# Rows loaded first, reciprocal roots on GpSimd, and the shift table built during the statistics, in a gated long-convolution and token-MLP kernel

## The chip, the cores and the metric

The kernel runs on one core of a Trainium2 chip. The metric is the device time of one execution in microseconds (us). "Span" is the time between the first and the last instruction in a profile; it is about 1.8 us shorter than the device time. The engines are TensorE (PE in the profile, with PEld for its weight loads), VectorE (DVE), ScalarE (ACT), GpSimd (POOL) and the DMA queues.

## The reference, cut to what matters

```python
# S = 2048 positions, D = 640 channels, F = 1536 hidden units, bf16
g = sigmoid((q * gate_w).sum(-1, keepdims=True))

# A: four shift taps, a product, a convolution over all S positions, a product
kv = shift4(k, shift_k) * v            # shift_k is (640, 4)
y  = irfft(rfft(pad(kv)) * rfft(pad(ssm_k)))[:S] + kv * ssm_D
a  = q * y

# B: layer norm over channels, then an MLP over positions
h = (q - mean(q)) / sqrt(var(q) + 1e-5)
u = gelu(einsum("bsd,sf->bdf", h, w1) + b1)
b = (einsum("bdf,fs->bds", u, w2) + b2).transpose(0, 2, 1)

out = g * a + (1 - g) * b
```

## The kernel before

The Fourier transforms are matrix products with a cosine and sine table `FTB`, which ScalarE makes at the start. The order of the work on TensorE: first come 40 transposes of the convolution filter (`transp`, first half of the positions), then 64 matmuls that transform it ("filter transforms", `fwd`, name W). The same follows for the second half. Then 80 matmuls apply the shift taps to `k`, and 128 transform the result ("convolution transforms", name A). Then come the rest of the MLP and the inverse transforms. Whenever nothing of this is ready, the matmuls of the first MLP layer (`m1`, priority 10^6, 384 of 128x320 in groups of 8) serve as filler. They need normalised rows `X`.

Instructions are ordered when the kernel is built, by a list scheduler that models the engines. A smaller `prio` goes first. PSUM is cut into four slots; the transforms may hold three, the MLP two. Each group of four transform matmuls ends in an eviction of 128x640 from PSUM by ScalarE, and only then is its slot free again.

```python
x_load(0)                                   # rows of q
for hk in range(2):
    ssm_load(hk)                            # filter rows
small(Drow...); small(rows... shift_k); small(rows... b2); small(rows... b1)
x_load(1); w1_load(0, 0); ssm_load(2); ssm_load(3); x_load(2); w1_load(0, 1); x_load(3)
# ...
SC.add("POOL", 1.3, lambda s: T.op("POOL", lambda e: e.tensor_copy(ro, ri), ...), name="taps")
# ... one PSUM tile takes b2, b1 and the turned taps (name "cst"), ScalarE takes them out (cc, cw)

def transp(h, p, kt):                       # 5 transposes, then one eviction
    # ...
    mms(vt, items, name="wtr")
    act(wT[:, hk, p, :], full, ACT.Copy, vt=vt, name="wT")

def fwd(src, h, p, dst, slot, scale, name, ...):
    for k2 in range(2):
        for c in range(2):
            # ... 4 matmuls of 128x320, then one eviction
            mms(vt, items, name=name)
            act(o, two, ACT.Copy, vt=vt, name=name + "e", **kw)

def ln_scale(a, b):                         # 1/sqrt by an integer guess and three Newton steps
    def emit(s):
        op(... ALU.add 1e-5); op(... logical_shift_right); op(... ALU.mult, ALU.add)
        for _ in range(3):
            op(scalar_tensor_tensor); op(tensor_tensor); op(scalar_tensor_tensor)
        op(... ALU.mult)
    return SC.add("DVE", 1.5, emit, ..., prio=0, name="rstd")

for h in range(2):
    for p in PORD:
        for kt in range(2):
            transp(h, p, kt)
    for p in PORD:
        fwd(srcW(h), h, p, C[h], p, 1.0 / 1024.0, "W", ...)
    if h == 0:
        for a, b in ((0, 8), (8, 16)):      # two halves of 8 row tiles
            for t in range(a, b):
                ln_tile(t // 4, t % 4)      # statistics: bn_stats twice, bn_aggr once
            ln_scale(a, b)                  # root
            ln_apply(a, b)                  # (x - mean) * rstd
        for g0 in (0, 5, 10, 15):           # the shift table KF, four multiplies
            tt("POOL", KF[...], V(cw, ...), V(m32, ...), ALU.mult)
        # ...
# ...
for ft in range(FT):                        # first MLP layer: the filler
    for hk in range(4):
        mms(vt, items, prio=10 ** 6 + 4 * ft + hk, name="m1")     # 8 matmuls
    g_ = act(GT[:, ft, :]..., two, ACT.Gelu_apprx_tanh, ..., vt=vt, prio=0, name="gelu")
```

## Time and profile before

| | before |
|---|---|
| time, median of 4 runs | 193.47 us (193.34 to 193.65) |
| span of the profiled run | 191.6 us |
| TensorE busy | 177.6 us, 93% |
| VectorE busy | 179.6 us, 94% |
| ScalarE busy | 116.3 us, 61% |

Two lines of the page come first: the busy time of each engine, and the shares of the chain of waits that ended last.

```profile
PE 177.6 (93%) x1403; PEld 130.0 (68%) x1403; DVE 179.6 (94%) x221; ACT 116.3 (61%) x187; POOL 26.8 (14%) x28
...
PE 58%; DVE 29%; ACT 10%; issue 1%; POOL 0%; DVEq 0%; POOLq 0%
```

Both TensorE and VectorE look full. The chain gives VectorE 29% of the span, and the change takes time from VectorE.

The next fence is VectorE's timeline around the first root. Its columns are start, duration, engine, line, operation, output and inputs, shapes and count; what an engine waited for stands in brackets.

```profile
13.90 0.84 DVE L862 BATCH_NORM_STATS2 stats<-X 128x6 f32<-128x320 bf16 x2
...
15.49 2.06 DVE L874 TENSOR_SCALAR sd<-mv 128x8 f32<-128x8 f32 x1
17.58 1.99 DVE L875 TENSOR_SCALAR rstd<-sd 128x8 int32<-128x8 int32 x1
19.61 1.99 DVE L876 TENSOR_SCALAR rstd<-rstd 128x8 int32<-128x8 int32 x1
21.63 0.17 DVE L878 SCALAR_TENSOR_TENSOR gth<-rstd 128x8 f32<-128x8 f32 x1
...
23.52 2.94 DVE L637 TENSOR_SCALAR X<-X,mv,rstd 128x640 bf16<-128x640 bf16 x8
...
41.47 2.94 DVE L637 TENSOR_SCALAR X<-X,mv,rstd 128x640 bf16<-128x640 bf16 x8
```

Three operations on eight numbers per partition take 2 us each, and the fourth takes 0.17 us. GpSimd's timeline shows what ran beside them:

```profile
4.98 3.31 POOL L776 COPY rows<-rows 20x512 bf16<-20x512 bf16 x1 [3.13 <-DMA rows<-in_A_shift_k_dram]
...
13.43 8.14 POOL L622 TENSOR_TENSOR KF<-cw,m 128x1120 bf16<-128x1120 bf16 x4 [5.15 <-ACT cw L666]
```

The four table multiplies take about 2.04 us each, from 13.43 to 21.57, and each of the three slow operations of VectorE ends with one of them. They took 2.0 us beside the multiplies, where the same three operations of the second root, with no multiply beside them, took 0.17 us each (37.56 to 38.14). The statistics keep their 0.42 us beside the first multiply (two in 0.84), as before it (two in 0.83 to 0.84). Why the ones take longer beside a multiply and the others don't, no run here shows.

The last view is a table of stretches. Each row has the stretch, its length, then busy time and count of instructions for PE, PEld, DVE, ACT and POOL, then TensorE's recorded clock, the DMA share and GB/s.

```profile
7.06:14.07 7.01, 5.30 (x49) 4.28 (x49) 7.01 (x24) 6.79 (x14) 1.86 (x2) 1.00 1.08 373
14.07:25.91 11.84, 11.51 (x72) 6.40 (x73) 11.36 (x25) 10.30 (x17) 7.50 (x4) 1.00 1.05 383
25.91:30.58 4.67, 4.06 (x50) 3.12 (x48) 4.67 (x13) 4.44 (x8) 0.00 (x0) 1.00 0.58 121
30.58:40.22 9.64, 9.64 (x65) 4.98 (x65) 9.23 (x32) 9.64 (x17) 0.87 (x1) 1.00 1.03 287
40.22:44.39 4.17, 4.15 (x82) 3.98 (x82) 4.17 (x10) 4.17 (x6) 0.00 (x0) 1.00 1.00 411
44.39:51.54 7.15, 5.87 (x47) 4.02 (x43) 7.15 (x9) 4.36 (x7) 0.00 (x0) 1.00 0.50 121
```

The rows are, in order: first transposes, first filter transforms with 8 filler matmuls, second transposes with 8, second filter transforms, shift taps, and 40 fillers with 2 convolution matmuls. The rest of the convolution transforms begins at 51.54. In a dense stretch of the second MLP product 320 matmuls take 43.63 us, 0.136 us each; a transpose or a shift-tap matmul takes about 0.054 us at full pace (80 shift-tap matmuls in 4.33 us). Call the length of a stretch minus its matmuls at these paces "lost". From 7.06 to 51.54 there are 186 large matmuls and 160 small ones, so 44.48 - 186 x 0.136 - 160 x 0.054 = 10.5 us are lost. This is the amount that the change could work on.

### The profile page before, as it was taken

The page shows a single profiled execution, that of the slowest core. Times are in us where ns is not written, and L with a number is a line of the kernel's source. Part 1 is how long each engine was busy: PE and PEld are TensorE (multiplying, and loading weights), DVE is VectorE, ACT ScalarE, POOL GpSimd, SP SyncE. Part 2 cuts the span into 40 slices and gives each one's busy share as a digit, 9 for nine tenths or more (in the row PEclk, how much of TensorE's full clock was granted, in tenths as well). Part 3 has the DMA queues.
Part 4 walks back from the last instruction along what each step waited for, and adds up shares of the span by engine and source line. Part 5 has one row for each costly group of instructions (what it writes and reads, how often), then busy time and mean ns, then how long its engine had stood idle before and what let it go on. Part 6 is the DMA issues. An engine that isn't in the chain of part 4 may idle for free.

```text
span 191.6 us, 3381 instructions
## 1 busy us (share of the span) xinstructions
PE 177.6 (93%) x1403; PEld 130.0 (68%) x1403; DVE 179.6 (94%) x221; ACT 116.3 (61%) x187; POOL 26.8 (14%) x28
## 2 busy tenths in 40 slices
PE   1469999999799999999999999999999999999993
PEld 0456465577466975777777777888888887777672
DVE  7999999999999999999999999999999996599764
ACT  4899979999399999998211221131313132874662
POOL 2619500100000405000002310405000000000000
PEclk9999999999999999999999999999999999999999
DMA  5999959994799199999929766698998900032233
GB/s 187 358 353 389 396 175 210 288 409 187 146 206 350 31 197 285 240 230 318 178 59 280 142 117 177 198 195 195 231 223 248 362 11 0 3 131 74 74 137 137
DMA packets 37295, 38.93 MB, mean 203 GB/s; under 512 B 15643, under 2 KB 32672, under 8 KB 37280
## 3 DMA queue, kind: packets, MB, share of 16 engines
q1 hardware_dynamic: 34464, 32.15, 54.9%
q0 software_dynamic: 2752, 6.55, 19.0%
q8 instruction: 11, 0.18, 0.3%
q14 instruction: 4, 0.03, 0.0%
q10 hardware_dynamic: 64, 0.01, 0.0%
HBM read 25.87 MB, written 2.62 MB: 149 GB/s over the span
## 4 chain that ended last, share of the span: by engine, by line
PE 58%; DVE 29%; ACT 10%; issue 1%; POOL 0%; DVEq 0%; POOLq 0%
PE pp L293 58%; DVE stats L862 6%; ACT C L666 3%; DVE C L622 3%; DVE SS L622 3%; DVE X L637 3%; ACT ksh L666 2%; ACT gq L666 2%; DVE pint L636 2%; DVE kp L735 2%; DVE vkv L622 1%; DVE pint L622 1%; ACT cgb L666 1%; DVE rstd L875 1%; DVE rstd L876 1%
## 5 line engine op out<-in xcount | busy, mean ns | idle before, releaser
L293 PE MATMUL pp<-X,ring 128*128 128x320 bf16 x384 | 53.8, 299 | 0.3 <-DVE X L637 0.3
L293 PE MATMUL pp<-GT,W 128*128 128x320 bf16 x384 | 53.3, 299 | 0.1
L293 PEld LDWEIGHTS pp<-GT,W 128*128 128x128 bf16 x384 | 43.5, 113 | 9.1 <-ACT cgb L666 0.4
L622 DVE TENSOR_TENSOR C<-C 128x2560 bf16<-128x2560 bf16 (+1 forms) x28 | 49.2, 1774 | 0.1
L293 PEld LDWEIGHTS pp<-X,ring 128*128 128x128 bf16 x384 | 37.1, 98 | 15.3 <-DVE X L637 0.7
L666 ACT ACTIVATE C<-pp 128x640 bf16<-128x640 f32 x64 | 39.3, 770 | 5.0 <-PE pp L293 4.8
L666 ACT ACTIVATE O<-pp,c,omg 128x640 bf16<-128x640 f32 (+1 forms) x17 | 14.5, 852 | 33.2 <-PE pp L293 33.2
L666 ACT ACTIVATE GT<-pp,cc 128x640 bf16<-128x640 f32 x12 | 9.6, 802 | 21.9 <-PE pp L293 21.8
L622 DVE TENSOR_TENSOR tm<-C,C 128x2560 bf16<-128x2560 bf16 (+2 forms) x12 | 20.2, 1709 | 0.5 <-DMA C<-tm 0.4
L293 PE MATMUL pp<-wT,FTB 128*128 128x320 bf16 x128 | 20.1, 311 | 0.6 <-ACT wT L666 0.4
L666 ACT ACTIVATE cgb<-pp,gg 128x640 bf16<-128x640 f32 x16 | 12.7, 792 | 7.7 <-PE pp L293 7.0
L293 PEld LDWEIGHTS pp<-wT,FTB 128*128 128x128 bf16 x128 | 10.8, 101 | 9.4 <-ACT C L666 4.4
L622 DVE TENSOR_TENSOR C<-tm 128x2560 bf16<-128x2560 bf16 (+1 forms) x12 | 14.9, 1265 | 0.1
L293 PE MATMUL pp<-C,GTB 128*128 128x320 bf16 x96 | 14.1, 299 | 0.0
L862 DVE BATCH_NORM_STATS2 stats<-X 128x6 f32<-128x320 bf16 x32 | 13.7, 472 | 0.0
L262 POOL DMA_DIRECT2D C<-C x6 | 7.4, 1390 | 43.5 <-DVE C L622 43.4
L666 ACT ACTIVATE gq<-gq 128x640 bf16<-128x640 bf16 x16 | 12.0, 777 | 0.0
L293 PEld LDWEIGHTS pp<-C,GTB 128*128 128x128 bf16 x96 | 9.0, 98 | 4.2 <-ACT O L666 0.8
L293 PE MATMUL pp<-ident,ssm 128*128 128x128 bf16 x80 | 8.0, 265 | 4.0 <-DMA ssm<-in_A_ssm_k_dram 3.4
L622 DVE TENSOR_TENSOR tm<-C,SS 128x5120 bf16<-128x5120 bf16 x4 | 11.1, 2818 | 0.0
L293 PE MATMUL pp<-vkv,FTB 128*128 128x320 bf16 x64 | 9.5, 300 | 1.3 <-DVE vkv L622 1.3
L293 PEld LDWEIGHTS pp<-ident,ssm 128*128 128x128 bf16 x80 | 6.5, 128 | 5.7 <-DMA ssm<-in_A_ssm_k_dram 4.2
(68 smaller groups left out, 182.8 us busy)
## 6 DMA issues: line engine op xcount, KB each, us to landing
ring<-in_B_w_dram SPq DMA_DIRECT2D x12, 512.0 KB, 9.5
W<-in_B_w_dram SPq DMA_DIRECT2D x8, 768.0 KB, 6.2
C<-C POOLq DMA_DIRECT2D x6, 640.0 KB, 10.0
X<-in_A_q_dram SPq DMA_DIRECT2D x4, 640.0 KB, 9.3
ssm<-in_A_ssm_k_dram SPq DMA_DIRECT2D x4, 640.0 KB, 8.9
kn<-in_A_k_dram SPq DMA_DIRECT2D x4, 640.0 KB, 9.3
out_dram<-O SPq DMA_DIRECT2D x7, 320.0 KB, 2.3
vkv<-in_A_v_dram SPq DMA_DIRECT2D x2, 640.0 KB, 4.6
```

The source lines that it names most:

```text
L262: ins = engobj.dma_start(out_ap, in_ap, accum_op=ALU.add, max_dma_last_dim=2560)
L293: ins = self.nc.tensor.matmul(ps_ap, lhsT=lhsT, rhs=rhs, start=start, stop=stop, skip_group_check=True)
L622: o_ = SC.add(eng, d, lambda s: T.op(eng, lambda e: e.tensor_tensor(o, a, b, op), [a, b], [o]), [a, b], [o], prio=prio, name="tt")
L636: return e.tensor_scalar(o, a, s1, None, op0=op0)
L637: return e.tensor_scalar(o, a, s1, s2, op0=op0, op1=op1)
L666: return T.op("ACT", lambda e: e.activation(o, src, func, **kw), rr + [src], ww)
L735: SC.add("DVE", 0.75, lambda s: T.op("DVE", lambda e: e.tensor_copy(ov, iv), [i[:, :, :]], [o[:, :, :]]), [i[:, :, :]], [o[:, :, :]], prio ...
L862: SC.add("DVE", 0.38, (lambda o, i: lambda s: T.op("DVE", lambda e: e.bn_stats(o, i), [i], [o]))(o, i), [i], [o])
L875: op(lambda e: e.tensor_scalar(yi, vi, 1, None, op0=ALU.logical_shift_right), [vi], yi)
L876: op(lambda e: e.tensor_scalar(yi, yi, -1.0, float(0x5F3759DF), op0=ALU.mult, op1=ALU.add), [yi], yi)
```

## The change

The intent is to give VectorE its 8 us back and to have normalised rows early, so that filler exists sooner. The rows of `q` are loaded before the weights. GpSimd computes the roots with a power operation. Twelve tiles, four of them of the second half, get their statistics before the first apply; the last four follow it, and then comes the second root. VectorE turns the taps. The taps get a PSUM tile of their own with top priority, so the table build on GpSimd runs beside the statistics, which kept their 0.42 us beside a multiply in before.

```diff
-            d = dve_dur(n, mode) + extra if eng == "DVE" else n / 900.0 + 0.3
+            d = dve_dur(n, mode) + extra if eng == "DVE" else n / 900.0 + 0.2
@@ loads
+        small(rows[0:20, 0, 0:128], dr(A_shift_k, ...), 5120, "QA")
+        small(rows[0:4, 1, :], dr(B_b2, ...), 4096, "QA")
+        small(rows[0:12, 2, 0:128], dr(B_b1, ...), 3072, "QA")
+        small(Drow[:, :], dr(A_ssm_D, ...), 1280, "QA")
         x_load(0)
         for hk in range(2):
             ssm_load(hk)
-        small(Drow...); small(rows... shift_k); small(rows... b2); small(rows... b1)
-        x_load(1)
-        w1_load(0, 0)
+        for hk in range(1, 4):
+            x_load(hk)
         ssm_load(2)
         ssm_load(3)
-        x_load(2)
+        w1_load(0, 0)
         w1_load(0, 1)
-        x_load(3)
@@ taps and table
-        SC.add("POOL", 1.3, lambda s: T.op("POOL", lambda e: e.tensor_copy(ro, ri), ...), name="taps")
+        SC.add("DVE", 0.6, lambda s: T.op("DVE", lambda e: e.tensor_copy(ro, ri), ...), prio=0, name="taps")
-        # b2, b1 and the taps in one PSUM tile: mms(vt, items, name="cst")
+        # the taps alone:                      mms(vt, items, prio=0, name="cst")
-            act(V(cw, ...), ..., name="cw")
+            act(V(cw, ...), ..., prio=0, name="cw")
+        def consts():                          # b2 and b1, called after the first transposes
@@ roots
         def ln_scale(a, b):
-            # 13 operations on VectorE (shown above)
+            n = b - a
+            ts("POOL", sd[:, a:b], mv[:, a:b, 1], 1e-5, None, ALU.add, prio=0)
+            tt("POOL", rstd[:, a:b], sd[:, a:b], V(cst, 1, [[0, n]]), ALU.pow, prio=0).dur = 1.05
+            return tt("POOL", sd[:, a:b], sd[:, a:b], rstd[:, a:b], ALU.mult, prio=0)
@@ order
-                for a, b in LNG:
-                    for t in range(a, b):
-                        ln_tile(t // 4, t % 4)
-                    ln_scale(a, b)
-                    ln_apply(a, b)
+                for t in range(12):
+                    ln_tile(t // 4, t % 4)
+                ln_scale(0, 8)
+                ln_apply(0, 8)
+                for t in range(12, 16):
+                    ln_tile(t // 4, t % 4)     # after the first apply
+                ln_scale(8, 16)
+                ln_apply(8, 16)
# cut: the lists that keep this order (lnlast), the same for the mixing products
```

More of the change, by code (lines that the diff above doesn't have):

```diff
@@ L748, in small @@
             dma(o, i, nbytes, stream=stream, **kw)
+        small(rows[0:20, 0, 0:128], dr(A_shift_k, 0, [[128, 20], [1, 128]]), 5120, "QA")
+        small(rows[0:4, 1, :], dr(B_b2, 0, [[512, 4], [1, 512]]), 4096, "QA")
+        small(rows[0:12, 2, 0:128], dr(B_b1, 0, [[128, 12], [1, 128]]), 3072, "QA")
+        small(Drow[:, :], dr(A_ssm_D, 0, [[0, 1], [1, D]]), 1280, "QA")
         x_load(0)
@@ L752, in _build @@
             ssm_load(hk)
-        small(Drow[:, :], dr(A_ssm_D, 0, [[0, 1], [1, D]]), 1280, "QA")
-        small(rows[0:20, 0, 0:128], dr(A_shift_k, 0, [[128, 20], [1, 128]]), 5120, "QA")
-        small(rows[0:4, 1, :], dr(B_b2, 0, [[512, 4], [1, 512]]), 4096, "QA")
-        small(rows[0:12, 2, 0:128], dr(B_b1, 0, [[128, 12], [1, 128]]), 3072, "QA")
-        x_load(1)
-        w1_load(0, 0)
+        for hk in range(1, 4):
+            x_load(hk)
         ssm_load(2)
         ssm_load(3)
-        x_load(2)
+        w1_load(0, 0)
         w1_load(0, 1)
-        x_load(3)
         T_PI = float(np.float32(math.pi * (1.0 - 1e-6)))
@@ L775, in _build @@
         ro, ri = rows[0:20, 3, :].rearrange("g (j q c) -> g j q c", j=4, q=4), V(rows, 0, [[1, 4], [0, 4], [4, 32]], pn=20)
-        SC.add("POOL", 1.3, lambda s: T.op("POOL", lambda e: e.tensor_copy(ro, ri), [ri], [ro]), [ri], [ro], name="taps")
+        SC.add("DVE", 0.6, lambda s: T.op("DVE", lambda e: e.tensor_copy(ro, ri), [ri], [ro]), [ri], [ro], prio=0, name="taps")
         PORD = (0, 2, 1, 3)
@@ L794, in _build @@
         items = []
-        for p in range(4):
-            items.append(((lambda s, p=p: s[:, 4 * p:4 + 4 * p]), V(rows, 512 + p, [[4, 128]], pn=4), ident[0:4, 0:4], True, True))
-        items.append(((lambda s: s[:, 16:28]), rows[0:12, 2, 0:128], ident[0:12, 0:12], True, True))
         for j in range(4):
             items.append(((lambda s, j=j: s[:, 512 + 20 * j:512 + 20 * j + 20]), rows[0:20, 3, 128 * j:128 * j + 128], ident[0:20, 0:20], True, True))
-        mms(vt, items, name="cst")
-        act(cc[:, :], lambda s: s[:, 0:28], ACT.Copy, vt=vt, name="cc")
+        mms(vt, items, prio=0, name="cst")
         for q in range(4):
-            act(V(cw, q, [[7, NG], [1, 4]], p0=32 * q, pn=32), (lambda s, q=q: s[32 * q:32 * q + 32, 512:592].rearrange("p (j g) -> p g j", j=4)), ACT.Copy, vt=vt, name="cw")
+            act(V(cw, q, [[7, NG], [1, 4]], p0=32 * q, pn=32), (lambda s, q=q: s[32 * q:32 * q + 32, 512:592].rearrange("p (j g) -> p g j", j=4)), ACT.Copy, vt=vt, prio=0, name="cw")
         b2f = V(cc, 0, [[1, 4], [4, 4]])
@@ L806, in _build @@
         ts("DVE", m32[:, :], dif2[:, :], 0.0, None, ALU.is_equal, mode=2)
+        def consts():
+            vt = _VT("cv")
+            items = []
+            for p in range(4):
+                items.append(((lambda s, p=p: s[:, 4 * p:4 + 4 * p]), V(rows, 512 + p, [[4, 128]], pn=4), ident[0:4, 0:4], True, True))
+            items.append(((lambda s: s[:, 16:28]), rows[0:12, 2, 0:128], ident[0:12, 0:12], True, True))
+            mms(vt, items, name="cst")
+            act(cc[:, :], lambda s: s[:, 0:28], ACT.Copy, vt=vt, name="cc")
         def transp(h, p, kt):
@@ L837, in tt @@
             def tt(*a):
-                return tt_(*a, prio=prio)
+                o_ = tt_(*a, prio=prio)
+                if prio is not None:
+                    o_.after.update(lnlast[-1:])
+                return o_
             def sl(h, s, n=1):
@@ L859, in ln_tile @@
             xs = X[:, hk, p, :]
+            ops = []
             for ci in range(2):
                 o, i = stats[:, t, 6 * ci:6 * ci + 6], xs[:, 320 * ci:320 * ci + 320]
-                SC.add("DVE", 0.38, (lambda o, i: lambda s: T.op("DVE", lambda e: e.bn_stats(o, i), [i], [o]))(o, i), [i], [o])
+                ops.append(SC.add("DVE", 0.38, (lambda o, i: lambda s: T.op("DVE", lambda e: e.bn_stats(o, i), [i], [o]))(o, i), [i], [o]))
             o, i = mv[:, t, :], stats[:, t, :]
-            SC.add("DVE", 0.12, (lambda o, i: lambda s: T.op("DVE", lambda e: e.bn_aggr(o, i), [i], [o]))(o, i), [i], [o])
+            ops.append(SC.add("DVE", 0.12, (lambda o, i: lambda s: T.op("DVE", lambda e: e.bn_aggr(o, i), [i], [o]))(o, i), [i], [o]))
+            return ops
         def ln_scale(a, b):
-            v, y, z, m_ = sd[:, a:b], rstd[:, a:b], gth[:, a:b], mv[:, a:b, 1]
-            yi = y.bitcast(I32)
-            vi = v.bitcast(I32)
-            def emit(s):
-                def op(fn, rr, w):
-                    T.op("DVE", fn, rr, [w])
-                op(lambda e: e.tensor_scalar(v, m_, 1e-5, None, op0=ALU.add), [m_], v)
-                op(lambda e: e.tensor_scalar(yi, vi, 1, None, op0=ALU.logical_shift_right), [vi], yi)
-                op(lambda e: e.tensor_scalar(yi, yi, -1.0, float(0x5F3759DF), op0=ALU.mult, op1=ALU.add), [yi], yi)
-                for _ in range(3):
-                    op(lambda e: e.scalar_tensor_tensor(out=z, in0=y, scalar=-0.5, in1=y, op0=ALU.mult, op1=ALU.mult), [y], z)
-                    op(lambda e: e.tensor_tensor(z, z, v, ALU.mult), [z, v], z)
-                    op(lambda e: e.scalar_tensor_tensor(out=y, in0=z, scalar=1.5, in1=y, op0=ALU.add, op1=ALU.mult), [z, y], y)
-                op(lambda e: e.tensor_tensor(v, v, y, ALU.mult), [v, y], v)
-            return SC.add("DVE", 1.5, emit, [m_], [v, y, z], prio=0, name="rstd")
+            n = b - a
+            ts("POOL", sd[:, a:b], mv[:, a:b, 1], 1e-5, None, ALU.add, prio=0)
+            tt("POOL", rstd[:, a:b], sd[:, a:b], V(cst, 1, [[0, n]]), ALU.pow, prio=0).dur = 1.05
+            return tt("POOL", sd[:, a:b], sd[:, a:b], rstd[:, a:b], ALU.mult, prio=0)
         def ln_apply(a, b):
@@ L886, in ln_apply @@
                 xs = X[:, t // 4, t % 4, :]
-                ts("DVE", xs, xs, mv[:, t, 0:1], rstd[:, t:t + 1], ALU.subtract, ALU.mult, mode=4, extra=0.16, prio=1)
+                o_ = ts("DVE", xs, xs, mv[:, t, 0:1], rstd[:, t:t + 1], ALU.subtract, ALU.mult, mode=4, extra=0.16, prio=1)
+                o_.after.update(lnlast[-1:])
         MIXP = 330
-        LNG = ((0, 8), (8, 16))
+        LNA = 8
+        lnlast = []
         KFP = (0, 5, 10, 15)
@@ L896, in _build @@
                     transp(h, p, kt)
+            if h == 0:
+                consts()
             for p in PORD:
@@ L899, in _build @@
             if h == 0:
-                for a, b in LNG:
-                    for t in range(a, b):
-                        ln_tile(t // 4, t % 4)
-                    ln_scale(a, b)
-                    ln_apply(a, b)
+                for t in range(8):
+                    ln_tile(t // 4, t % 4)
+                for t in range(8, 12):
+                    ln_tile(t // 4, t % 4)
+                lnlast.append(SC.ops[-1])
+                ln_scale(0, LNA)
+                ln_apply(0, LNA)
+                lnlast.append(SC.ops[-1])
+                for t in range(12, 16):
+                    for o_ in ln_tile(t // 4, t % 4):
+                        o_.after.update(lnlast[-1:])
+                ln_scale(LNA, 16)
+                ln_apply(LNA, 16)
+                lnlast.append(SC.ops[-1])
                 for g0 in KFP:
```

## The prediction

> **What bounds it now.** The timeline shows TensorE without a gap from 51.5 to 188.4 us; by the table of stretches it is busy 136.4 of those 136.9 us, at a granted clock of 1.00. 320 matmuls of the second MLP product take 43.6 us there (0.136 us each), so that stretch is TensorE at its pace. The last 3.2 us are ScalarE, VectorE and the output DMA. What can be won lies before 51.5 us. Matmuls started there: 80 weight transposes (about 0.054 us each), 128 filter transforms, some 58 MLP matmuls, 80 of the shift convolution: about 34 us of work at those paces in the 44.5 us since 7.06 us, when the first filter rows landed. So some 10 us are lost, nearly all because ScalarE evacuates slowly (0.61 us per transform group, 0.63 per transpose group) or because normalised rows, the filler, are not there.
>
> VectorE is busy 94% and never waits from 1 to 112 us. In its timeline the first root (adds, integer steps, three Newton rounds on 128x8) takes 8.0 us, 15.5 to 23.5: three of its 13 operations last 2.0 us each, against 0.17 us in the second root. They end as GpSimd's four shift-table multiplies end (2.06 us each, 13.4 to 21.6). Batch statistics beside the first multiply kept their 0.43 us. [...]
>
> **The change, on VectorE.** Removed: 8.0 us and 2.5 us of roots. Added: the shift-tap turn, estimated 0.6 us from the 0.82 us strided key copies. GpSimd's 3.3 us turn, behind which a small operation lasted 0.67 us, goes. The table build moves to about 8.7 to 17 us, under statistics, and costs nothing. The first half's root is hidden behind four more statistics tiles (0.86 us each); the second's is exposed, I guess 1 to 2 us (no power on GpSimd is in this trace), partly filled by a key turn. First apply: 18.6 instead of 23.5 us; second: 27.5 instead of 41.5. VectorE runs 8 to 9 us ahead.
>
> **On ScalarE.** The four table evictions (1.0 us) move into its idle time near 6.3 us. Its gap at 24.8 to 26.1 and the 3.2 us wait before 52.0 mostly close.
>
> **On the critical path.** The convolution's transforms now start at 51.5, after a VectorE product; ScalarE's own work (about 39.5 us from 7.4) would allow 47 to 48. First-layer matmuls must fill the gaps as well as the 5.4 us they filled at 44.4 to 49.8. They can start near 20 us, when the weights (now later in the queue) land, but until about 28 only 16 exist, so the transposes near 24 to 28 stay half empty. I expect 3 to 5 of the 10 us back. VectorE's 8 to 9 us of lead is mostly not time: TensorE stays the limit, with the same 3 us tail.
>
> **Predicted 189.6 us, 187.4 to 191.8 eight times in ten.** Faster by over 2%: 0.51; within 2%: 0.47; slower: 0.02.
>
> **To check.** Statistics still 0.43 us beside the table build; no 2 us tiny operations; both applies begin near 18.6 and 27.5; convolution transforms begin at 46 to 49; TensorE dense until 183 to 185; tail near 3 us.
>
> **What would make it wrong.** GpSimd's power taking several microseconds, [...]; the fixed instruction order making an engine wait for a DMA that lands later than planned (weights after all rows); TensorE fillers starving ScalarE, so that only 1 us comes back; or VectorE's lead letting the inverse transforms finish early and shorten the tail as well, for a gain above 6 us.

## The result, and the profile after

| | before | after |
|---|---|---|
| time, median of 4 runs | 193.47 us | 191.88 us (191.66 to 192.32) |
| span of the profiled run | 191.6 us | 190.1 us |
| convolution transforms begin in earnest | 51.54 | 52.96 |
| large matmuls done before that | 186 | 200 |
| lost on TensorE from the first transpose to there | 10.5 us | 9.8 us |
| end of TensorE | 188.38 | 187.00 |

The ratio of after to before is 0.992, with a 95% interval of 0.990 to 0.994. A ratio is the mean time of one kernel's runs over that of the other's of the same rounds, so it isn't quite the ratio of the medians quoted here. Executions over 1.5% slower than the fastest of the same kernel are left out of the means. The kernel became 0.8% faster; 2% had been given a chance of one half. All outputs are right. The page of after:

```profile
PE 175.9 (93%) x1403; PEld 131.2 (69%) x1403; DVE 170.3 (90%) x196; ACT 116.8 (61%) x187; POOL 33.5 (18%) x33
...
PE 86%; ACT 9%; DMA 3%; issue 0%; SPq 0%; DVE 0%
```

VectorE lost 9.3 us of busy time, and it left the chain. TensorE's share of the chain rose from 58% to 86%, and yet the span fell by only 1.5 us. VectorE's timeline after:

```profile
13.77 0.82 DVE L870 BATCH_NORM_STATS2 stats<-X 128x6 f32<-128x320 bf16 x2
...
18.99 2.94 DVE L637 TENSOR_SCALAR X<-X,mv,rstd 128x640 bf16<-128x640 bf16 x8 [0.26 <-POOL rstd L622]
...
28.99 2.94 DVE L637 TENSOR_SCALAR X<-X,mv,rstd 128x640 bf16<-128x640 bf16 x8 [2.11 <-POOL rstd L622]
...
45.28 0.23 DVE L636 TENSOR_SCALAR gpre<-mv,gws 128x16 f32<-128x16 f32 x1 [3.41 <-ACT gq L666]
```

The first apply came 4.5 us earlier and the second 12.5 us. Part of the lead turned into waiting: 2.11 us for the second root, and 3.41 us at 45.28 for a ScalarE sum queued behind the first Gelu. GpSimd's timeline after:

```profile
8.83 8.14 POOL L622 TENSOR_TENSOR KF<-cw,m 128x1120 bf16<-128x1120 bf16 x4 [6.97 <-ACT wT L666]
16.95 0.25 POOL L636 TENSOR_SCALAR sd<-mv 128x8 f32<-128x8 f32 x1
17.27 1.68 POOL L622 TENSOR_TENSOR rstd<-sd,cst 128x8 f32<-128x8 f32 x1
...
33.94 6.53 POOL L967 COPY KT<-KT 128x20 bf16<-128x20 bf16 x1 [4.70 <-DMA KT<-kp]
```

The table is built from 8.83 to 16.97, beside statistics that still take 0.41 us each. The power operation took 1.68 us on 128x8. VectorE's part of the change therefore worked as intended. The stretches of after, in the same order as before:

```profile
7.28:14.43 7.15, 4.87 (x47) 3.77 (x48) 7.15 (x25) 6.39 (x10) 5.60 (x3) 0.98 1.04 401
14.43:26.01 11.58, 11.58 (x72) 7.14 (x73) 11.28 (x37) 9.58 (x17) 4.64 (x5) 0.86 1.07 364
26.01:31.00 4.99, 4.30 (x50) 3.22 (x49) 2.88 (x9) 4.75 (x9) 2.11 (x3) 1.00 1.07 183
31.00:44.44 13.44, 12.38 (x88) 8.04 (x89) 10.84 (x10) 12.76 (x21) 6.53 (x1) 1.00 0.98 330
44.44:48.62 4.18, 4.16 (x83) 3.98 (x81) 3.34 (x5) 3.99 (x7) 0.00 (x0) 1.00 0.01 2
48.62:52.96 4.34, 4.34 (x36) 3.12 (x33) 4.34 (x4) 3.77 (x8) 0.00 (x0) 1.00 1.01 139
```

Look at the second filter transforms, the row that starts at 31.00. They now hold 24 fillers (88 matmuls, not 64). That is 3.3 us of work at 0.136 us each, and the row grew from 9.64 to 13.44 us, by 3.8 us. Lost time in this row rose from 0.9 to 1.5 us (13.44 - 88 x 0.136). In the last row the loss went from 1.4 us to nothing. The first three rows hardly moved: 4.85 to 5.0, 2.05 to 1.8, 1.4 to 1.75. From 7.28 to 52.96 there are 200 large and 160 small matmuls, so 45.68 - 27.2 - 8.64 = 9.8 us are lost.

The end of TensorE moved by 1.38 us, and the sum closes. It lost 0.7 us less before the convolution transforms and 0.90 us less after them (136.84 us from 51.54 to 188.38 in before, 134.04 us from 52.96 to 187.00 in after, where 14 large matmuls fewer are left: 136.84 - 134.04 - 14 x 0.136), and it started 0.22 us later. Of the 0.90 us, 0.32 us is one wait for an eviction at 72.90, gone in after; the rest is spread out, and I did not trace it.

The timeline of ScalarE in after shows what the fillers did to it:

```profile
25.12 1.90 ACT L666 ACTIVATE C<-pp 128x640 bf16<-128x640 f32 x3 [0.65 <-PE pp L293]
...
35.17 4.28 ACT L666 ACTIVATE C<-pp 128x640 bf16<-128x640 f32 x7 [0.65 <-PE pp L293]
39.47 1.28 ACT L666 ACT_TABLE_LOAD   x1
40.77 0.79 ACT L666 ACTIVATE GT<-pp,cc 128x640 bf16<-128x640 f32 x1
41.46 3.07 ACT L666 ACTIVATE C<-pp 128x640 bf16<-128x640 f32 x5
```

Each time TensorE runs 8 fillers (1.09 us) in the middle of the transforms, ScalarE runs dry for 0.65 us. A transform group takes TensorE 4 x 0.136 = 0.545 us and ScalarE about 0.605 us, so ScalarE is the slower one, but only by a tenth, and at most three slots lie between them. Also, the four early filler groups complete the first hidden block in the middle of these evictions, so its Gelu now stands there with its table load: 2.07 us from 39.47 to 41.46. TensorE then waits once:

```profile
42.21 1.31 PE L293 MATMUL pp<-wT,FTB 128*128 128x320 bf16 x8 [1.06 <-ACT C L666]
...
52.96 4.01 PE L293 MATMUL pp<-vkv,FTB 128*128 128x320 bf16 x28
```

In before it waited elsewhere:

```profile
51.54 3.75 PE L293 MATMUL pp<-vkv,FTB 128*128 128x320 bf16 x26 [1.28 <-DVE vkv L622]
```

A second thing stands in the row that starts at 14.43: a recorded clock of 0.86, where before had 1.00. These are the durations of the transform matmuls that ran between 14.5 and 18 us, as shortest, median and longest in ns, first in before and then in after:

```profile
L293 PE MATMUL pp<-wT,FTB x22: 299/299/474, 14.1 to 17.9; 128*128 128x320 bf16 x22
```

```profile
L293 PE MATMUL pp<-wT,FTB x15: 299/474/475, 14.4 to 17.9; 128*128 128x320 bf16 x15
```

Where the matmuls last 474 ns, TensorE runs at half pace: a group of four then takes 1.06 us instead of 0.545. In both kernels the filter transforms begin at half pace, until about 16.2 in before and 17.7 in the profiled run of after. Evictions are then 1.06 us apart (15.72 and 16.78 in after) and not 0.605, so each such group costs 0.45 us. The column of the clock shows this in after only; in before, 474 ns stands beside a clock of 1.00. The half pace, called the cold start below, ended at different times in different runs: 16.2 and 17.7 us here, about 17.0 and 19.3 us in two profiles below. What starts and what ends it, no run here shows; that more matmuls ahead of it would keep TensorE "warm", at full pace, is a guess, which two experiments below try.

### The profile page after: what moved, and what is told of

Its sections match the earlier page's. It is cut to its first block, busy times and chain, and to the rows that moved or that the text cites. A ratio compares the mean times of both kernels' runs of the same rounds, so it can differ in the third digit from the quotient of the medians.

```text
span 190.1 us, 3364 instructions
## 1 busy us (share of the span) xinstructions
PE 175.9 (93%) x1403; PEld 131.2 (69%) x1403; DVE 170.3 (90%) x196; ACT 116.8 (61%) x187; POOL 33.5 (18%) x33
## 4 chain that ended last, share of the span: by engine, by line
PE 86%; ACT 9%; DMA 3%; issue 0%; SPq 0%; DVE 0%
PE pp L293 86%; ACT wT L666 4%; DMA ssm<-in_A_ssm_k_dram 3%; ACT C L666 3%; ACT FTB L666 1%; ACT L666 1%; ACT GT L666 0%; ACT O L666 0%; SPq L267 0%; DVE O L622 0%
## 5 line engine op out<-in xcount | busy, mean ns | idle before, releaser
L666 ACT ACTIVATE O<-pp,c,omg 128x640 bf16<-128x640 f32 (+1 forms) x17 | 14.5, 852 | 35.0 <-PE pp L293 32.5
L293 PEld LDWEIGHTS pp<-wT,FTB 128*128 128x128 bf16 x128 | 11.9, 102 | 9.0 <-ACT C L666 3.0
L666 ACT ACTIVATE wT<-pp 128x640 bf16<-128x640 f32 x16 | 10.0, 723 | 1.1 <-PE pp L293 1.1
L262 POOL DMA_DIRECT2D C<-tm x4 | 3.5, 866 | 37.8 <-DVE C L622 37.8
```

The source lines that it names most:

```text
L262: ins = engobj.dma_start(out_ap, in_ap, accum_op=ALU.add, max_dma_last_dim=2560)
L293: ins = self.nc.tensor.matmul(ps_ap, lhsT=lhsT, rhs=rhs, start=start, stop=stop, skip_group_check=True)
L666: return T.op("ACT", lambda e: e.activation(o, src, func, **kw), rr + [src], ww)
```

## The experiments

Twelve builds ran in three batches, one of them after itself. Each batch had its own runs of before: 193.38 us in the first, 193.61 us in the second, 193.36 us in the third (medians of 11). The expectations name theories by letters, and each says in its text what it expects. H is that TensorE and ScalarE, which hand groups to each other, set the pace before the convolution; VectorE's lead is then worth only the waits that TensorE had for it, and moving the table build gives nearly the whole gain. Its rivals are F, V and L: that the gain comes from rows normalised earlier (the filler), that VectorE's lead as such is time, or that loading rows first delayed filters or weights and ate part of the gain. (In the later expectation of the kernel with eight evictions moved, V is that VectorE has too little slack.) G is that the Gelu amid the evictions eats the gain, C that the cold start of TensorE does, and S that ScalarE's evictions set the pace before the convolution, so that fillers there only displace them. Every edit also lets the scheduler reorder the instructions behind it, so a run tests an edit together with its new order.

### The table part alone

Before, with the small loads first, the taps turned on VectorE, the table's own PSUM tile and its priority. Roots, order of statistics and large loads are those of before.

```diff
 # before, plus:
+ small(rows... shift_k), small(rows... b2), small(rows... b1), small(Drow...)   ahead of x_load(0)
- SC.add("POOL", 1.3, ..., name="taps")
+ SC.add("DVE", 0.6, ..., prio=0, name="taps")
+ mms(vt, <taps only>, prio=0, name="cst"); act(... prio=0, name="cw"); consts() after the first transposes
```

> Kernel before with one part of the change: small loads first, taps turned on VectorE, shift table built under the statistics; roots stay on VectorE, loads of rows as before. Theory H (the head is set by TensorE and ScalarE handing groups to each other, VectorE's lead is worth only the waits that TensorE had for it, 1.5 us before the convolution transforms and about 0.5 us elsewhere): the first root falls from 8.0 to about 2.5 us, that wait vanishes, 191.5 to 192.5 us, that is nearly all of the whole change. Rival F (the gain of the whole change comes from rows normalised earlier, as fillers): 193 us or more.

Measured: 191.19 us (191.17 to 192.13), ratio 0.9899 (0.9885 to 0.9914). VectorE's timeline around the first root:

```profile
15.32 1.66 DVE L879 TENSOR_SCALAR sd<-mv 128x8 f32<-128x8 f32 x1
17.02 0.17 DVE L880 TENSOR_SCALAR rstd<-sd 128x8 int32<-128x8 int32 x1
...
19.31 2.93 DVE L637 TENSOR_SCALAR X<-X,mv,rstd 128x640 bf16<-128x640 bf16 x8
```

One operation lasts 1.66 us, until the table's end at 16.95, and the other twelve take 0.17 us each. The first root lasts 4 us instead of 8.0, the convolution transforms begin at 50.95, and TensorE does not wait for VectorE there. This small part of the change gives all of its gain, as H says. It does not exclude F: the shorter root also brought the first apply from 23.52 to 19.31, and 24 fillers instead of 16 ran before the last filter eviction. The run without early fillers, below, bears on F. The profile fell on the slowest of the five runs (192.13 us), with half pace until about 19.3.

### The roots back on VectorE

```diff
 # after, with ln_scale of before (13 operations on VectorE)
```

> Kernel after with the roots back on VectorE (13 tiny operations each). The first root now falls under the end of the table build. Theory H: VectorE loses 5 to 7 us of its lead, tiny operations last up to 2 us until the build ends near 17 us, 0.17 us after that; the time stays within 0.6 us of the kernel after (191.3 to 192.5). Rival V (VectorE's lead is time): 194 us or more.

Measured: 191.53 us (191.36 to 192.04), ratio 0.9911 (0.9898 to 0.9924), where after had 0.992. GpSimd's power operations are worth nothing that these runs can measure. H holds; V falls.

### The large loads in their old order

```diff
 # after, with:
+ x_load(1); w1_load(0, 0); ssm_load(2); ssm_load(3); x_load(2); w1_load(0, 1); x_load(3)
- x_load(1); x_load(2); x_load(3); ssm_load(2); ssm_load(3); w1_load(0, 0); w1_load(0, 1)
```

> Kernel after with the order of the large loads as before (rows interleaved with filters and weights). Theory H (the head is paced by ScalarE and TensorE): the second half of the rows is normalised 1 to 3 us later, nothing else; 191.2 to 192.3 us, as the kernel after. Rival L (rows first delayed the filters or weights and ate the gain): 190.9 us or less.

Measured: 192.08 us (191.34 to 192.67), ratio 0.992 (0.9901 to 0.994), the same as after. L falls: loading rows first cost nothing that these runs can measure, and it gained nothing.

### The first Gelu after the filter transforms

```diff
 # after; wlast = the last eviction of the filter transforms
             if ft == 0:
+                g_.after.add(wlast)
```

> Kernel after with the first Gelu held back until the last weight-transform eviction, so that the table load (1.28 us) and that Gelu (0.79 us) no longer stand in the middle of ScalarE's evictions, and VectorE does not wait 3.4 us for the sum behind it. Theory G (the table load in the middle costs TensorE its 1.06 us wait at 41.2 us): that wait is gone, 190.7 to 191.2 us. Rival: only moved, TensorE waits or idles elsewhere for as long, 191.5 to 192.2 us.

Measured: 192.13 us (191.46 to 192.34), ratio 0.9926 (0.9912 to 0.994). The wait of 1.06 us at 42.21 is gone, and a wait of 1.09 us for the same Gelu appeared at 44.67. The table load took 1.28 us, and the Gelu began 0.01 us after it. So the Gelu costs ScalarE its 2.07 us in either place, and G as recorded falls. A Gelu behind the shift-tap evictions too is not tried alone.

### TensorE kept warm, first attempt

```diff
 # after; after each of the first four transposed filter tiles:
+ mms(vt_dm, [(s[:, 0:320], ident, wT tile[0:320])] * 3, prio=10 ** 7)     # never read
```

> Kernel after with 12 extra matmuls (three 128x320 after each of the first four weight transposes of the first half, into a free PSUM slot, never read) that only keep TensorE busy between 9 and 14 us; outputs unchanged. Theory C (the granted clock of 0.50 from 14.3 to 17.7 us, after a 1.4 us gap of TensorE, ate part of the gain): clock 1.00 in that stretch, first evictions of the transforms 0.6 us apart instead of 1.06, 190.3 to 191.0 us. Rival: the dip falls where ScalarE or the loads set the pace anyway: within 0.4 us of the kernel after.

Measured: 192.49 us (fast runs 191.02 to 192.63), ratio 0.9937 (0.9914 to 0.996), and one run of 655.61 us. The profile fell on that run. Its convolution transforms between 100 and 200 us:

```profile
L293 PE MATMUL pp<-vkv,FTB x64: 767/767/924, 147.6 to 188.1; 128*128 128x320 bf16 x64
```

All large matmuls of that run last so long, for its whole 654 us, and 52 of them took 26.99 us, 0.52 us each: about a quarter of the usual pace. The recorded clock is 1.00. That run explains nothing about the change. The experiment is inconclusive: there is no profile of a fast run, and the extra matmuls may cost time themselves.

### TensorE kept warm, second attempt

```diff
 # after; 30 matmuls of ident x ident, 18 that wait for the taps' rows,
 # and 8 after each of the first four transposed tiles, all 128x128
+ mms(vt_dm, [(s[:, 0:128], ident, ident)] * 30, prio=10 ** 7)             # never read
```

> Kernel after with extra matmuls that are never read: 30 of 128x128 before the filter rows land, 18 more after the tap transposes, 8 after each of the first four transposed tiles. Theory C (TensorE is at half pace, 474 instead of 299 ns a matmul, in the first 2 to 4 us of the filter transforms, and by chance longer or shorter, which makes the runs scatter by 1 us): 299 ns from 14.4 us on, evictions 0.6 us apart from the first, 190.2 to 191.1 us in all runs, scatter under 0.4 us. Rival: time and scatter as the kernel after (191.7 to 192.3 us).

Measured: 192.35 us (190.87 to 193.6), ratio 0.9941 (0.9906 to 0.9975). The profiled run, 191.0 us, was warm, without a transform matmul at half pace:

```profile
L293 PE MATMUL pp<-wT,FTB x23: 299/299/299, 15.0 to 18.0; 128*128 128x320 bf16 x23
```

In it the evictions were 0.6 us apart from the first. Of the other five runs one took 190.87 us and four took 192.23 to 193.6, so the scatter did not go, and C's forecast for the time failed. C is at most half supported: the one warm profile goes with a fast run (after's own best was 191.63 in ten runs). The filter transforms began at 15.01 in it, later than in after (14.43), so the extra matmuls have a cost too, and I can't say how much of the change's time the cold start is.

### Half of the second transposes evicted on VectorE

```diff
 # after
-            act(wT[:, hk, p, :], full, ACT.Copy, vt=vt, name="wT")
+            if h == 1 and kt == 1:
+                evac_dve(wT[:, hk, p, :], full, vt, prio=0)
+            else:
+                act(wT[:, hk, p, :], full, ACT.Copy, vt=vt, name="wT")
```

> Kernel after with four of the eight transposed-filter evictions of the second half moved from ScalarE to VectorE, which waits 2.1 us for the root just then. Theory S (in the head ScalarE's evictions are the pace): ScalarE does 2.4 us less between 26 and 31 us, the transposes there take about 3 us instead of 5, the time is 189.0 to 190.4 us. Rival: no gain beyond scatter (191.3 us or more), because TensorE or VectorE sets the pace there.

Measured: 190.78 us (190.19 to 191.22), ratio 0.9857 (0.984 to 0.9875). It is faster than both kernels, though by a little less than I expected. The second transposes and transforms end at 40.70, with the Gelu behind them, and the time lost before the convolution transforms is 8.4 us by the same sum (43.15 us from 7.11 to 50.26, 192 large matmuls). VectorE took 0.77 to 0.78 us for each eviction (1.56 and 1.54 us for two).

The gain did not come where S put it. The second transposes lasted 4.73 us (25.82 to 30.55), not 3, against 4.99 in after. Of the 1.4 us, 1.15 us lie in the second filter transforms, whose evictions were not moved. They now hold 8 fillers and no Gelu, where after has 24 fillers and the Gelu, because VectorE's second apply came later:

```profile
34.57 2.94 DVE L637 TENSOR_SCALAR X<-X,mv,rstd 128x640 bf16<-128x640 bf16 x8 [2.12 <-POOL rstd L622]
```

So the evictions on VectorE bring a gain, but whether by relieving ScalarE, as S says, or by moving fillers and the Gelu out of these transforms, this run does not separate.

### Half of all transposes evicted on VectorE

```diff
 # after
-            if h == 1 and kt == 1:      # of the kernel above
+            if kt == 1:
```

> The same with four of eight evictions of the first half too, under the statistics. Theory S: the filter transforms start 1.5 to 2.5 us earlier than 14.4 us, both gains add: 187.5 to 189.3 us, although VectorE carries about 6 us more. Rival V (VectorE is needed for the statistics there, its lead is worth time): no better than with the second half alone.

Measured: 193.05 us (192.5 to 193.11), ratio 0.9971 (0.9959 to 0.9983). The filter transforms began at 14.13, hardly earlier than after's 14.43, and not the expected 1.5 to 2.5 us earlier. VectorE became the late one: the second apply moved to 38.74, and the products that the inverse transforms need came late. The same inverse transforms on TensorE, first here, then in after:

```profile
162.04 4.58 PE L293 MATMUL pp<-C,GTB 128*128 128x320 bf16 x32
```

```profile
156.10 4.58 PE L293 MATMUL pp<-C,GTB 128*128 128x320 bf16 x32
```

By then the matmuls of the second MLP product, which should fill the end, were used up. TensorE ended at 186.3 and the tail was 4.8 us instead of 3.1. VectorE's slack is finite: in these two schedules four evictions fit and eight don't.

### After once more

```diff
 # after, unchanged
```

> The kernel after once more, as a companion of the three runs beside it: 191.6 to 192.4 us. The time that TensorE spends at half pace (474 ns a matmul) after 14.4 us should differ from the first profile by chance.

Measured: 191.81 us (191.63 to 192.53), ratio 0.9926 (0.9912 to 0.9939), as in the first result. In its profile the half pace of the filter transforms ended near 17.0 us instead of 17.7, by chance as expected, and the convolution transforms began at 52.85.

### No fillers before the last filter eviction

```diff
 # after; wlast = the last eviction of the filter transforms
-                mms(vt, items, prio=10 ** 6 + 4 * ft + hk, name="m1")
+                mms(vt, items, prio=10 ** 6 + 4 * ft + hk, name="m1").after.add(wlast)
```

> Kernel after in which no first-layer matmul may start before the last filter-transform eviction: none of the 32 fillers before 42 us. They are 4.4 us of TensorE time at 0.136 us each and have to run later. Theory S (in the transform stages a filler of 1.1 us makes ScalarE run dry by about 0.65 us, so fillers there buy little): the last filter-transform eviction comes 3 us or more earlier than at 44.5 us, and the time is within 1 us of the kernel after. Rival (the fillers fill time that was really free, as my prediction had it): 4 us slower, 195.5 us or more.

Measured: 192.49 us (192.13 to 193.19), ratio 0.9964 (0.9949 to 0.9979), 0.7 us slower than after in the same rounds. ScalarE's timeline without the fillers:

```profile
16.20 9.83 ACT L666 ACTIVATE C<-pp 128x640 bf16<-128x640 f32 x16 [0.66 <-PE pp L293]
25.74 5.06 ACT L666 ACTIVATE wT<-pp 128x640 bf16<-128x640 f32 x8
30.42 9.93 ACT L666 ACTIVATE C<-pp 128x640 bf16<-128x640 f32 x16
40.29 4.75 ACT L666 ACTIVATE ksh<-pp 128x1024 bf16<-128x1024 f32 x6
```

And TensorE's line where the convolution transforms begin:

```profile
48.90 4.01 PE L293 MATMUL pp<-vkv,FTB 128*128 128x320 bf16 x28
```

ScalarE doesn't pause from 16.20 to 45. It ends the filter transforms at 40.35, where after ended them near 44.5; 2.07 us of that is the Gelu, which moved behind them. The convolution transforms begin at 48.90, 4.06 us earlier than in after, with 32 filler matmuls fewer behind them. These 32 are 32 x 0.136 = 4.35 us of TensorE work. So in after they cost 4.06 us of delay for 4.35 us of work: TensorE loses 10.2 us without them and 9.8 us with them. This is the decisive run. Had the fillers gone into time that was really free, taking them away would have cost some 4 us; it cost 0.7 us. S holds for fillers and their Gelu together; their shares of the delay are not separated. It does not hold everywhere alike: the second transposes lose 2.5 us without their 8 fillers (4.69 us for 40 matmuls) and 1.7 us with them in after, so these 8 filled mostly free time.

For F this run says: without early fillers the kernel is still 0.7 us faster than before by the ratio, half of the change's gain. The other half goes with the early fillers, of which before had 16 and after 40 ahead of the last filter eviction.

### The table part with the four evictions on VectorE

```diff
 # the table part alone, with the edit of "half of the second transposes"
+            if h == 1 and kt == 1:
+                evac_dve(wT[:, hk, p, :], full, vt, prio=0)
```

> The part with the table alone (roots on VectorE, loads as before) plus the four second-half evictions on VectorE. Theory H and S together: the two gains add, 190.0 to 191.0 us, no slower than the same evictions in the kernel after (190.8 us). Rival (with more work on VectorE the roots on GpSimd begin to pay): over 0.7 us slower than those 190.8 us.

Measured: 191.42 us (190.89 to 191.76), ratio 0.9895 (0.9882 to 0.9908). It is no better than the table part alone (0.9899), so the two gains did not add here. ScalarE ended the filter transforms earlier (41.56 instead of 43.4), but only 16 instead of 24 fillers had run by then, and the half pace lasted to 18 us in its profile. It is 0.64 us slower by the medians than the same edit on after. In the table part alone the Gelu already stood behind the filter transforms, so the missing gain fits the second reading of that edit. The 0.64 us hint that the early rows and GpSimd's roots pay once VectorE has more to do, but the two come from different batches, and it is inconclusive.

### The sine table ahead of the evictions

```diff
 # after with the four evictions on VectorE, and
-                act(wT[:, hk, p, :], full, ACT.Copy, vt=vt, name="wT")
+                act(wT[:, hk, p, :], full, ACT.Copy, vt=vt, name="wT").after.add(sins[2])
```

> Kernel after with the four second-half evictions on VectorE and the last two sine activations put ahead of the first transposed-filter eviction, into ScalarE's idle 0.8 us at 7.2 us. Theory S: ScalarE gets the 0.8 us, the filter transforms start near 13.7 instead of 14.5 us, 189.7 to 190.5 us, faster than all others. Rival: half-paced matmuls eat it, 190.6 us or more.

Measured: 191.99 us (191.34 to 192.56), ratio 0.9925 (0.991 to 0.994). The transforms began at 14.55, no earlier than after's 14.43, and the Gelu again stood before the last filter eviction (its table load at 41.62), with 16 fillers in the second transforms. It is worse than the kernel that it started from.

| kernel | median us | ratio to before |
|---|---|---|
| after, once more | 191.81 | 0.9926 |
| table part alone | 191.19 | 0.9899 |
| after, roots on VectorE | 191.53 | 0.9911 |
| after, no early fillers | 192.49 | 0.9964 |
| after, four evictions on VectorE | 190.78 | 0.9857 |
| after, eight evictions on VectorE | 193.05 | 0.9971 |

The other six, with ratios from 0.9895 to 0.9941, stand in their sections.

## Why the prediction was right or wrong

- **What bounds the kernel, and that VectorE's lead is mostly not time: right.** VectorE lost 9.3 us of busy time and 29 points of the chain, and the time fell by 1.6 us. The prediction said that TensorE stays the limit with the same tail; the tail is 3.1 us against 3.2.
- **Statistics beside the table build, and no 2 us operations: right.** They took 0.41 us each, and the small operations between them 0.18 us. Moving the table alone, with the earlier first apply that follows from it, gave the whole gain.
- **Times of the applies: nearly right.** Predicted 18.6 and 27.5, measured 18.99 and 28.99. The second root was exposed for 2.11 us, just above the guess of 1 to 2. The power took 1.68 us.
- **ScalarE's table evictions moved into idle time: they did, and no gain shows in the traces.** The 1.0 us ran at 6.2 to 7.2. Then ScalarE waited 0.8 us for TensorE, and its sine tables came between the first filter evictions. The first transform eviction came at 15.72, in before at 15.36.
- **"First-layer matmuls must fill the gaps ... I expect 3 to 5 of the 10 us back": this step failed.** The term was mis-sized: 0.7 us came back before the convolution transforms (10.5 to 9.8). By the table of stretches 4.85 of the 10.5 us were lost before 14.07, where by the prediction's own times no normalised row existed (first apply at 18.6, first fillers near 20), so the 3 to 5 us had to come from the other 5.7. And the prediction treated TensorE's empty time as room into which ready matmuls could be poured. In these stages TensorE's empty time follows from ScalarE's evictions, with three slots between. A filler there makes ScalarE run dry, 0.65 us for 1.09 us of filler where it was traced, and the transforms that follow come later by about as much. Taking 32 fillers out showed it: 4.35 us of work, 4.06 us of delay, with the 2.07 us of their Gelu in it. The prediction named "TensorE fillers starving ScalarE, so that only 1 us comes back" among the things that would make it wrong, and this is what came.
- **Convolution transforms at 46 to 49, TensorE dense until 183 to 185: wrong, as a consequence.** They began at 52.96, and TensorE ended at 187.00. The later start itself is no loss, since 14 more large matmuls had run by then.
- **"A granted clock of 1.00": too trusting.** The statement was made of the dense stretch, where it holds. But I took the column at its word for the early stages too, and never read the 474 ns that stood in before's own trace. Half pace at the start of the filter transforms is part of the 10 us, which no filler can win: TensorE was busy for 2.12 of the 2.13 us from 14.07 to 16.20 in before. By the estimate of 0.45 us a group, it is about 0.9 us in before (two groups) and 1.4 us in the profiled run of after (three). It varies from run to run.

What stays open: how much of the change's time the cold start took, since neither attempt at warming separated it; where 0.6 us of TensorE's gain after the convolution transforms began came from; how the fillers and the first Gelu share the delay; by which way four evictions on VectorE gain; and whether GpSimd's roots pay once VectorE carries evictions.

## What to carry to other kernels

Idle time of an engine that trades small groups with another through a few buffers belongs to the pair: before counting it as room for filler, ask which of the two is slower and what that one does while the filler runs. A little operation of VectorE cost ten times as much next to GpSimd's multiplies as it cost alone (2.0 us against 0.17), while batch statistics next to them kept their pace (0.41 us each), and moving the multiplies under the statistics was the whole gain of a larger change here: so look at what runs beside GpSimd work, and at how long it takes there. And time freed on an engine that isn't the limit brought nothing here until it was given work of another engine: four evictions given to VectorE brought 1.1 us more (how is open), and eight took back more than that.

## Single operations and the clock column, as measured here

- Batch statistics took 0.41 us each beside GpSimd multiplies of 2.04 us (after), where small VectorE operations took 2.0 us beside them instead of 0.17 (before).
- In after a GpSimd copy of 128x20 lasted 6.53 us beside back-to-back products of 1.4 us on VectorE; in before the same copy took 0.87 us. Why, no run here shows.
- A recorded clock of 1.00 stood beside matmuls of 474 ns, and in one run beside 767 ns for 654 us, the whole run. So the clock column alone doesn't tell the pace; the durations beside it do.
- A table load took 1.28 us, and the next activation began 0.02 us after its end (after, at 40.77).
- A power operation on GpSimd took 1.68 us for 128x8, where a multiply of the same shape took 0.20 us.
